# The front of a one-core attention and MLP kernel: four maximum products and six projection products in turn, and what stands behind the first closing

## The chip, the cores and the metric

The kernel runs on one core of a Trainium2 chip. The metric is device time in microseconds of one execution. The core has TensorE (matrix products, called PE in the profile), VectorE (DVE), ScalarE (ACT) and GpSimd (POOL); SyncE (SP) issues most transfers. The kernel writes the order of instructions in each of the five queues out by hand, and no scheduler changes it.

## The reference, cut to what matters

One block: a layer norm with shift and scale from a condition vector `c`, attention with 32 heads of 16 numbers that share one set of keys and values, a gated residual, a second layer norm, and an MLP with a tanh GELU. 2048 rows of 512 numbers, all in float32.

```python
mod = (_silu(c) @ w_mod).reshape(c.shape[0], 6, 1, -1)
sa, ca, ga, sb, cb, gb = (mod[:, 0], mod[:, 1], mod[:, 2], mod[:, 3], mod[:, 4], mod[:, 5])
h = _layernorm(x, axis=-1) * (1 + ca) + sa
q = ... (x @ wq) as 32 heads of 16; k = x @ wk; v = x @ wv
scores = jnp.einsum("bhqd,bkd->bhqk", q, k) * (Dh ** -0.5)
p = _softmax(scores, axis=-1)
x = x + ga * (p v as 512 numbers a row) @ wo
h = _layernorm(x, axis=-1) * (1 + cb) + sb
x = x + gb * (_gelu(h @ w1 + b1) @ w2 + b2)
```

## The kernel before, in words

**The attention.** A unit `u` is one block of 256 query rows with four heads. For each unit the scores are computed twice. The first time, 32 products `m<-ks,qst` (L512) give scores of 128 queries against 512 keys; VectorE reduces each to its row maximum (`mx<-m`, L517). When the 32 reduces of a unit are done, the unit is closed by `put_max`: one more reduce (`mm`, L565), a transpose (`turned`, L566), the gathering of the maxima into rows (`mt`, L560), the split of these into a high and a low part (`mh`, `ml`), and transfers that put both as rows 48 and 49 (and 112 and 113) of the unit's query tile `qst` (L555). The second time, products `e<-qst,ks` (L617) give the same scores with the maximum already subtracted, ScalarE takes the exponential (`p<-e`, L621), and `acc<-p,va` (L638) multiplies by the values. The products of units 0 and 1 are taken in the order of `FIRST_MAX`, over both units; unit 0 is complete with the 48th product. That is the first closing. The loop over units starts with an `e` of unit 0, so it needs the first rows to have landed.

**Halves of the array.** `m` and `e` contract over 64 rows. A product with `s` = 0 uses the upper half of the array and one with `s` = 1 the lower, so two of them run side by side. The projections contract over all 128 rows.

**The front.** Ahead of the loop the 2048 rows are normalised, transposed and modulated block by block of 512 (`tp`, `h`, `bigH`, `bigL`: "heads 1" to "heads 3"). From each block come the keys and values (`kps`, 12 products in four groups of three: "keys 1" to "keys 3"). ScalarE copies the keys out twice (`kv_out`, L401) and the values once (`vt`, L402), VectorE computes the keys' low part (`low_k`, L407), ScalarE copies this once more (`repeat_k`, L411), and `v_out` (L419, L420) transposes the values. "q 1" is the second projection of queries (`qps`, 12 products), "rows" the four sets of late modulation rows (`modl`, L297, 8 instructions each), "wq 1" to "wq 3" the split of query weights (L342, L343), "load" the loading of unit 2's queries.

The order of all this around the maximum products is a table, `SLOTS`. Each entry is a number of maximum products followed by names of steps. This loop reads it:

```python
for n, *names in SLOTS:
    chunk(n)
    for name in names:
        next(work[name])
```

Four more maximum products follow the table, so that 56 are issued when the loop begins.

**PSUM banks.** The kernel divides its PSUM into eight tiles of 512 numbers a partition. The maximum products take turns in three with the tag `m`. Three more, `e0` to `e2`, are given out in rotation by `ebank()`; in the front the transposes `tp` and `vps` use them, and in the loop the `e` products, beginning with `e0`. The remaining two have the tags `v` (`kps` of blocks 0 to 2, `qps` of "q 1") and `x` (`kps` of block 3, `modl`). A product waits until the engine that empties its bank has done so, and what stands behind it in TensorE's order waits with it.

**Idle products.** `keep_warm` issues products whose result nobody reads. `WARM` holds how many at four places; the last is straight ahead of the loop (L1410).

Of the kernel before, what the change touches and what calls it, by code (L numbers as in the profile page):

```python
# [14 lines left out]
P = 128  # L15
# [29 lines left out]
WARM = (4, 16, 2, 5)  # L45
# [4 lines left out]
def raw(ap):  # L50
    return ap.bitcast(F32)
# [3 lines left out]
def adaln_mqa_mlp(  # L55
# [230 lines left out]
    def keep_warm(n, **place):  # L286

        for k in range(n):
            if k == 0 or not place:
                ps = psum.tile([P, BQ], F32, name=f"idle{len(idles)}", **(place or dict(tag="m", bufs=3)))  # L290
                idles.append(ps)
            nc.tensor.matmul(ps, wkH[:, 0, :], wkH.rearrange("p k n -> p (k n)"), start=True, stop=True)
# [98 lines left out]
    def kv_products(b):  # L391
        hH, hL = hts[b]
        kps[b] = psum.tile([P, BQ], F32, name=f"kps{b}", tag="x" if b == 3 else "v")
        return mm3(kps[b], [(wkH[:, k, :], wkL[:, k, :], hH[:, k, :], hL[:, k, :]) for k in range(KD)], 3)

    def kv_out(b):
        ps = kps[b]
        cols = slice(b * BQ, (b + 1) * BQ)
        vt = pro.tile([P, BQ], F32, name=f"vt{b}", tag="vt", bufs=2)
        for r in range(2):  # L400
            nc.scalar.copy(ks[64 * r:64 * r + 48, cols], ps[64 * r:64 * r + 48, :])  # L401
        nc.scalar.copy(vt[32:64, :], ps[32:64, :])  # L402
        vts[b] = vt

    def low_k(b):
        cols = slice(b * BQ, (b + 1) * BQ)
        nc.vector.tensor_tensor(out=ks[32:48, cols], in0=kps.pop(b)[32:48, :], in1=raw(ks[32:48, cols]), op=ALU.subtract)  # L407
# [128 lines left out]
    def put_max(u, mx):  # L536
# [13 lines left out]
        def send():  # L550
            for s in range(2):
                for r, src in ((48, mh), (49, ml)):
                    dst = qst[64 * s + r:64 * s + r + 1].rearrange("p j (t n) -> p (j t) n", n=P)
                    ring = nc.scalar if u == 0 and s else nc.sync
                    ring.dma_start(out=raw(dst), in_=raw(src[2 * T * s:2 * T * (s + 1), :].unsqueeze(1)))  # L555
            placed.add(u)
# [7 lines left out]
        def reduce():  # L564
            nc.vector.tensor_reduce(out=mm[:, :4 * T], in_=mx, axis=AX.X, op=ALU.max)  # L565
            nc.vector.transpose(out=turned, in_=mm)  # L566
            later(MAX_WAIT[0], gather)
            later(MAX_WAIT[1], send)
# [676 lines left out]
    def k_products(b):  # L1245
        for _ in kv_products(b):
            pass
# [84 lines left out]
    run(keys(0))  # L1332
    low_k(0)
# [19 lines left out]
    for n, *names in SLOTS:  # L1353
        chunk(n)
        for name in names:
            next(work[name])
# [53 lines left out]
    keep_warm(WARM[3], tag="e2", bufs=1)  # L1410
# [172 lines left out]
```

## Time and profile before

| | us |
|---|---|
| three timed runs | 1555.87, 1556.47, 1556.48 (median 1556.47) |
| the profiled execution | 1555.99 |
| its span, first to last instruction | 1554.1 |
| PE busy | 1537.9 (99%) |
| DVE busy | 1398.3 (90%) |
| ACT busy | 1230.4 (79%) |
| POOL busy | 683.7 (44%) |
| first maximum reduce of the stretch that the change rewrites, start | 48.68 |
| first `e` product of the loop, start | 75.14 |

In the profile's rows a time stands first, then a duration; `x8` is the number of instructions that a row merges, and the brackets hold the engine's idle time before the row and what ended it. The duration of a merged row runs from the start of the first to the end of the last. Instructions of one engine can overlap at their ends, so rows that follow each other start a little closer together than their durations say. The granted clock of TensorE is 1.000 over the whole execution.

### The profile page before, as it was taken

To read this page: it belongs to the slowest core of one execution; us is meant where nothing else is said; L and a number is where in the kernel's file an instruction comes from. 1 tells how busy PE (TensorE), PEld (TensorE's weight loads), DVE (VectorE), ACT (ScalarE), POOL (GpSimd) and SP (SyncE) were. 2 spreads that over 40 slices of the span, in tenths; PEclk is the share of its full clock that TensorE was granted. 3 is DMA by queue.
4 is the path that set the end of the run, shared out by engine and by line. 5 is a ranking of instruction groups with operands and counts; after the bars stand their busy time and mean duration, and the time that the engine had idled before them with its cause. 6 is when DMAs were issued, how large, how long until landed. Compare 5 with 4: busy or idle time off the path is not lost.

```text
span 1554.1 us, 41556 instructions
## 1 busy us (share of the span) xinstructions
PE 1537.9 (99%) x16405; PEld 954.4 (61%) x16405; DVE 1398.3 (90%) x2488; ACT 1230.4 (79%) x2401; POOL 683.7 (44%) x1206
## 2 busy tenths in 40 slices
PE   7999999999999999999999999999999999999999
PEld 4455555567655665557655676556655676566658
DVE  7999999999999999999999999999999999999814
ACT  5577778788877887788877888788877888778874
POOL 5535432867422571246521563235711574046511
PEclk9999999999999999999999999999999999999999
DMA  7226412413030220303112120302212230203141
GB/s 240 102 89 199 151 57 81 130 51 97 18 105 26 72 68 28 103 19 109 33 51 79 56 87 16 111 26 88 68 30 73 60 101 25 87 28 99 48 150 48
DMA packets 84215, 120.85 MB, mean 78 GB/s; under 512 B 21342, under 2 KB 57438, under 8 KB 83764
## 3 DMA queue, kind: packets, MB, share of 16 engines
q1 hardware_dynamic: 84004, 118.18, 23.7%
q8 instruction: 130, 2.13, 0.6%
q14 instruction: 65, 0.53, 0.1%
q10 hardware_dynamic: 16, 0.00, 0.0%
HBM read 90.87 MB, written 26.74 MB: 76 GB/s over the span
## 4 chain that ended last, share of the span: by engine, by line
PE 86%; DVE 8%; issue 3%; POOL 2%; DMA 1%; ACT 0%; SPq 0%; POOLq 0%; DVEq 0%
PE acc L638 29%; PE m L512 23%; PE e L617 16%; PE w1ps L198 8%; DVE mx L517 6%; PE w2ps L198 2%; PE w2ps L188 2%; DMA xt<-in_A_x_dram 1%; PE w1ps L188 1%; PE wops L198 1%; PE tp L198 1%; PE qps L198 1%; PE kps L165 1%; DVE st L823 0%; DVE x L816 0%
## 5 line engine op out<-in xcount | busy, mean ns | idle before, releaser
L517 DVE TENSOR_REDUCE mx<-m 128x1 f32<-128x512 f32 x2048 | 1270.6, 682 | 86.6 <-PE m L512 65.1
L621 ACT ACTIVATE p<-e 128x512 f32<-128x512 f32 x2048 | 1098.8, 598 | 255.1 <-PE e L617 112.0
L512 PE MATMUL m<-ks,qst 64*128 64x512 f32 x2048 | 836.7, 429 | 2.0 <-DVE mx L517 0.6
L617 PE MATMUL e<-qst,ks 64*128 64x512 f32 x2048 | 740.2, 412 | 0.0
L638 PE MATMUL acc<-p,va 128*32 128x256 f32 x8192 | 548.0, 385 | 0.0
L512 PEld LDWEIGHTS m<-ks,qst 64*128 64x128 f32 x2048 | 368.2, 184 | 205.1 <-DVE mx L517 173.5
L617 PEld LDWEIGHTS e<-qst,ks 64*128 64x128 f32 x2048 | 359.6, 184 | 89.3 <-ACT p L621 62.5
L638 PEld LDWEIGHTS acc<-p,va 128*32 128x32 f32 x8192 | 214.0, 109 | 213.9 <-issue 110.9
L198 PE MATMUL w1ps<-h2H,w1t 64*128 64x256 f32 x1232 | 235.5, 287 | 0.0
L560 POOL TENSOR_SCALAR mt<-turned 8x32 f32<-8x32 f32 x256 | 53.1, 208 | 399.9 <-DVE turned L566 387.9
L198 PEld LDWEIGHTS w1ps<-h2H,w1t 64*128 64x128 f32 x1232 | 186.0, 185 | 28.9 <-DVE mx L517 14.8
L198 PE MATMUL w1ps<-h2L,w1t 64*128 64x256 f32 x616 | 169.3, 275 | 0.0
L198 PE MATMUL w2ps<-w2H,gH 64*128 64x512 f32 x274 | 120.3, 439 | 0.0
L198 PEld LDWEIGHTS w1ps<-h2L,w1t 64*128 64x128 f32 x616 | 114.1, 185 | 0.0
L198 PE MATMUL w2ps<-w2L,gH 64*128 64x512 f32 x274 | 107.5, 392 | 0.0
L198 PE MATMUL w2ps<-w2H,gL 64*128 64x512 f32 x274 | 106.9, 390 | 0.0
L975 POOL TENSOR_SCALAR tt<-tt 128x256 f32<-128x256 f32 x77 | 31.0, 402 | 131.5 <-ACT tt L974 96.5
L140 POOL TENSOR_TENSOR gL<-z,gH 128x256 fp32r<-128x256 f32 x77 | 57.0, 741 | 6.4
L976 POOL TENSOR_TENSOR tt<-tt,z 128x256 f32<-128x256 f32 x77 | 56.7, 736 | 6.4
L986 POOL TENSOR_TENSOR z<-tt,z 128x256 f32<-128x256 f32 x77 | 56.4, 732 | 6.0
L985 POOL TENSOR_TENSOR tt<-tt,z 128x256 f32<-128x256 f32 x77 | 56.5, 733 | 0.0
L198 PEld LDWEIGHTS w2ps<-w2H,gH 64*128 64x128 f32 x274 | 50.4, 184 | 6.7 <-DVE ot L1038 2.5
(193 smaller groups left out, 1503.5 us busy)
## 6 DMA issues: line engine op xcount, KB each, us to landing
w1t<-dw SPq DMA_DIRECT2D x82, 512.0 KB
qst<-dq SPq DMA_DIRECT2D x384, 32.0 KB
do<-oc SPq DMA_DIRECT2D x62, 128.0 KB
dw<-w1s SPq DMA_DIRECT2D x11, 512.0 KB
xt<-in_A_x_dram SPq DMA_DIRECT2D x4, 1024.0 KB
dq<-qH SPq DMA_DIRECT2D x16, 256.0 KB
dq<-qL SPq DMA_DIRECT2D x16, 256.0 KB
x<-in_A_x_dram SPq DMA_DIRECT2D x8, 512.0 KB
```

Of the source, the lines that this page charges most:

```text
L140: eng_l.tensor_tensor(out=dst_l, in0=src, in1=raw(dst_h), op=ALU.subtract)
L188: nc.tensor.matmul(ps, a, b_, start=first_, stop=last_)
L198: ins = nc.tensor.matmul(ps, a[rows], b_[rows], start=first_ and s == 0, stop=last_ and s == 1)
L512: nc.tensor.matmul(m, qsts[u][rows, j, t * P:(t + 1) * P], ks[rows, kc * 512:(kc + 1) * 512], start=True, stop=True)
L517: nc.vector.tensor_reduce(out=self.mx[u][:, i, kc:kc + 1], in_=m, axis=AX.X, op=ALU.max)
L560: nc.gpsimd.tensor_scalar(out=mt[:, g:g + 32], in0=turned[g:g + 4 * T, :], scalar1=1.0, scalar2=0.0, op0=ALU.mult, op1=ALU.add)
L617: nc.tensor.matmul(e, ks[rows, kt * P:(kt + 1) * P], rhs, start=True, stop=True)
L621: ins = nc.scalar.activation(dst, e, AF.Exp, scale=0.25)
L638: ins = nc.tensor.matmul(accs[u][32 * cidx:32 * cidx + 32, :], va[:, kt, :], rhs, start=kt == 0, stop=kt == NKT - 1)
L976: nc.gpsimd.tensor_tensor(out=tt, in0=tt, in1=z, op=ALU.mult)
L985: nc.gpsimd.tensor_tensor(out=tt, in0=tt, in1=z, op=ALU.mult)
L986: nc.gpsimd.tensor_tensor(out=z, in0=tt, in1=z, op=ALU.add)
```

## The change

It rewrites the table `SLOTS` and five things around it.

- An entry may now hold several numbers among its names. From the first keys of block 2 on, four maximum products stand in a row and then six projection products, where before two and three alternated.
- In these entries (from the 12th on, but for the last two) the odd ones of the maximum products, counted from 0 (`s` = 1), take a bank of the rotation `e0` to `e2` instead of one of the three `m`.
- The values `v 2` and `v 3`, all four sets of `rows`, and the query weights `wq 2` and `wq 3` stand behind the 48th product. Six products then follow inside the table in place of four, and two behind it in place of four.
- The copy `vt` of blocks 1 to 3 moves from `kv_out` to behind `repeat_k`, and is now called `keep_v`.
- The first unit's rows (`place_first`): two of the four pieces of `mt` are copied by ScalarE and two by GpSimd, `mh` is made by ScalarE and `ml` by GpSimd. Each of `mh` and `ml` is put in place by one transfer of two rows from SP, where there were four of one row, two of them from ScalarE.
- The five idle products ahead of the loop are gone (the last number of `WARM` is 0).

TensorE's order at the start of the rewritten stretch, in the program before (`kps` is a product of keys 2, `m_u_j_t_kc_s` a maximum product of the unit whose last numbers it shows):

```order
L165 MATMUL kps_646<-bigH,wkH 128x512
L165 MATMUL kps_646<-bigH,wkL 128x512
L165 MATMUL kps_646<-bigL,wkH 128x512
L512 MATMUL m_1_0_1_0_650<-ks,qst_157 128x512
L512 MATMUL m_1_0_1_1_653<-ks,qst_157 128x512
L165 MATMUL kps_646<-bigH,wkH 128x512
L165 MATMUL kps_646<-bigH,wkL 128x512
L165 MATMUL kps_646<-bigL,wkH 128x512
L512 MATMUL m_1_1_1_0_659<-ks,qst_157 128x512
L512 MATMUL m_1_1_1_1_662<-ks,qst_157 128x512
```

And in the changed program:

```order
L517 MATMUL m_1_0_1_0_646<-ks,qst_157 128x512
L517 MATMUL m_1_0_1_1_649<-ks,qst_157 128x512
L517 MATMUL m_1_1_1_0_652<-ks,qst_157 128x512
L517 MATMUL m_1_1_1_1_655<-ks,qst_157 128x512
L166 MATMUL kps_658<-bigH,wkH 128x512
L166 MATMUL kps_658<-bigH,wkL 128x512
L166 MATMUL kps_658<-bigL,wkH 128x512
L166 MATMUL kps_658<-bigH,wkH 128x512
L166 MATMUL kps_658<-bigH,wkL 128x512
L166 MATMUL kps_658<-bigL,wkH 128x512
```

The two pairs of maximum products moved together and stand ahead of the first projection products of keys 2.

TensorE's order around the first closing before; `m_1_1_3_1` is unit 0's last maximum product (`modl` are mod rows, `vps` the transposes of values, `qps` the last products of "q 1"):

```order
L165 MATMUL qps_1_754<-h0L,wqH 128x512
L297 MATMUL modl<-wml_0_378,csb 32x512 x2
L297 MATMUL modl<-wml_1_379,csb 32x512 x2
L512 MATMUL m_1_0_3_0_798<-ks,qst_157 128x512
L512 MATMUL m_1_0_3_1_801<-ks,qst_157 128x512
L419 MATMUL vps_804<-ident,vt_730 128x32 x4
L512 MATMUL m_1_1_3_0_814<-ks,qst_157 128x512
L512 MATMUL m_1_1_3_1_817<-ks,qst_157 128x512
L297 MATMUL modl<-wml_0_382,csb 32x512 x2
L297 MATMUL modl<-wml_1_383,csb 32x512 x2
L512 MATMUL m_0_0_2_0_842<-ks,qst_158 128x512
L512 MATMUL m_0_0_2_1_845<-ks,qst_158 128x512
```

And now:

```order
L166 MATMUL qps_1_754<-h0L,wqH 128x512
L517 MATMUL m_1_0_3_0_787<-ks,qst_157 128x512
L517 MATMUL m_1_0_3_1_790<-ks,qst_157 128x512
L517 MATMUL m_1_1_3_0_793<-ks,qst_157 128x512
L517 MATMUL m_1_1_3_1_796<-ks,qst_157 128x512
L424 MATMUL vps_815<-ident,vt_699 128x32 x4
L299 MATMUL modl<-wml_0_378,csb 32x512 x2
L299 MATMUL modl<-wml_1_379,csb 32x512 x2
L517 MATMUL m_0_0_2_0_826<-ks,qst_158 128x512
L517 MATMUL m_0_0_2_1_829<-ks,qst_158 128x512
L424 MATMUL vps_832<-ident,vt_752 128x32 x4
L299 MATMUL modl<-wml_0_382,csb 32x512 x2
```

The first set of mod rows and a set of value transposes left the way to the closing; both value transposes and all mod rows follow it.

ScalarE's order at the same place before (`turned` holds the transposed maxima, `q_0_1` and `qH` belong to "q 1", `modl_sb` is the copy of the mod rows):

```order
L135 CAST qH_1_785<-q_0_1_787 128x512
L420 COPY va<-vps_804 128x4x16
L342 CAST wqH<-wqf 128x4x64 x2
L555 DMA qst_157<-mh_824 1x4x128
L555 DMA qst_157<-ml_825 1x4x128
L342 CAST wqH<-wqf 128x4x64 x2
L1364 COPY modl_sb<-modl 128x512
```

And now:

```order
L136 CAST qH_1_779<-q_0_1_781 128x512
L564 COPY mt_802<-turned_799 8x32 x2
L136 CAST mh_803<-mt_802 8x128
L425 COPY va<-vps_815 128x4x16
L425 COPY va<-vps_832 128x4x16
L344 CAST wqH<-wqf 128x4x64 x4
L1387 COPY modl_sb<-modl 128x512
```

ScalarE lost two transfers and gained three small copies, ahead of the value copies and the weights.

The diff, without the parts that only rename:

```diff
-         (2, "heads 3"), ..., (0, "keys 2"), (2, "keys 2"), (2, "keys 2"), (2, "keys 2"),
+         (4, "keys 2", "keys 2"), (4, "keys 2", "keys 2"), (2, "low 2", 2, "k 2", "keys 3", "keys 3", "v 1", "wq 1"), ...
...
+WIDE = 11
-WARM = (4, 16, 2, 5)
+WARM = (4, 16, 2, 0)
...
     def kv_out(b):
-        vt = pro.tile([P, BQ], F32, name=f"vt{b}", tag="vt", bufs=2)
         for r in range(2):
             nc.scalar.copy(ks[64 * r:64 * r + 48, cols], ps[64 * r:64 * r + 48, :])
-        nc.scalar.copy(vt[32:64, :], ps[32:64, :])
-        vts[b] = vt
...
+    def keep_v(b):
+        vts[b] = pro.tile([P, BQ], F32, name=f"vt{b}", tag="vt", bufs=2)
+        nc.scalar.copy(vts[b][32:64, :], kps[b][32:64, :])
 
     def repeat_k(b):
         cols = slice(b * BQ, (b + 1) * BQ)
         nc.scalar.copy(ks[96:112, cols], raw(ks[32:48, cols]))
+        if b:
+            keep_v(b)
...
+        def place_first():
+            for i in range(2):
+                for g, piece in ((32 * i, lambda d, s: nc.scalar.copy(d, s)),
+                                 (64 + 32 * i, lambda d, s: nc.gpsimd.tensor_scalar(out=d, in0=s, ...))):
+                    piece(mt[:, g:g + 32], turned[g:g + 4 * T, :])
+
+            def send_row(r, src):
+                dst = qst[r:r + 65:64].rearrange("p j (t n) -> p (j t) n", n=P)
+                nc.sync.dma_start(out=raw(dst), in_=raw(src.unsqueeze(1)))
+
+            split(mh, ml, mt, nc.scalar, nc.gpsimd, lambda: send_row(48, mh))
+            send_row(49, ml)
+            placed.add(u)
...
         def reduce():
             nc.vector.tensor_reduce(out=mm[:, :4 * T], in_=mx, axis=AX.X, op=ALU.max)
             nc.vector.transpose(out=turned, in_=mm)
+            if u == 0:
+                place_first()
+                return
...
+    wide = [False]
     def chunk(n):
         for _ in range(n):
-            mp.step(mp.done % 2)
+            mp.step(mp.done % 2, **(ebank() if wide[0] and mp.done % 2 else {}))
...
-    for n, *names in SLOTS:
-        chunk(n)
-        for name in names:
-            next(work[name])
+    for i, slot in enumerate(SLOTS):
+        wide[0] = WIDE <= i < len(SLOTS) - 2
+        for part in slot:
+            if isinstance(part, int):
+                chunk(part)
+            else:
+                next(work[part])
```

More of the change, by code (lines that the diff above doesn't have):

```diff
@@ L284, in adaln_mqa_mlp, with keep_warm @@
     idles = []
-    def keep_warm(n, **place):
+    def keep_warm(n, src=None, **place):
+        src = wkH.rearrange("p k n -> p (k n)") if src is None else src
         for k in range(n):
@@ L291, in keep_warm @@
                 idles.append(ps)
-            nc.tensor.matmul(ps, wkH[:, 0, :], wkH.rearrange("p k n -> p (k n)"), start=True, stop=True)
+            nc.tensor.matmul(ps, src[:, :P], src, start=True, stop=True)
     def mod_rows(ps, k, wm):
@@ L1332, in adaln_mqa_mlp @@
     run(keys(0))
+    keep_v(0)
     low_k(0)
@@ L1408, in end_step @@
                 put_off(rest(units[u][0], units[u][0] == len(blocks) - 1))
-    keep_warm(WARM[3], tag="e2", bufs=1)
+    keep_warm(WARM[3], bigH[:, 0, 0, :], tag="v")
     behind = None
```

9 lines of the change are left out of this document (3 added, 6 removed), and 8 rows, old and new, of the table SLOTS.

## The prediction

> **What bounds the kernel now.** I read the chain that ended last first, then busy time by stage, then VectorE and TensorE in order of time through the front.
>
> ```profile
> PE 86%; DVE 8%; issue 3%; POOL 2%; DMA 1%; ACT 0%; SPq 0%; POOLq 0%; DVEq 0%
> ```
> ```profile
> 48.17:69.56 21.39, 21.11 (x92) 10.11 (x91) 19.12 (x30) 9.90 (x21) 10.13 (x11) 1.00 0.06 22
> ...
> 69.56:75.14 5.58, 5.26 (x29) 1.92 (x27) 5.33 (x10) 0.74 (x2) 2.81 (x10) 1.00 0.08 23
> ...
> 84.70:1450.00 1365.30, 1364.52 (x15160) 846.27 (x15160) 1280.62 (x2245) 1114.49 (x2172) 614.30 (x1091) 1.00 0.23 73
> ```
>
> In the second fence the columns are the stretch, its length, then busy time and instructions of PE, PEld, DVE, ACT and POOL, the granted clock, the DMA share and GB/s. From 84.70 to 1450 us TensorE idles under 1 us: that is the long loop, and the change leaves its instructions as they are. So the change can only move the start of that loop. The part it edits runs from 48.17 to about 84.7 us. There TensorE is busy 21.11 of 21.39 us and VectorE 19.12: two engines near their limit, each waiting a little for the other. VectorE in order of time:
>
> ```profile
> 48.68 5.27 DVE L517 TENSOR_REDUCE mx<-m 128x1 f32<-128x512 f32 x8 [0.51 <-PE m L512]
> 54.04 0.68 DVE L407 TENSOR_TENSOR ks<-kps,ks 16x512 fp32r<-16x512 f32 x1
> ...
> 54.76 5.21 DVE L517 TENSOR_REDUCE mx<-m 128x1 f32<-128x512 f32 x8
> 60.06 0.68 DVE L407 TENSOR_TENSOR ks<-kps,ks 16x512 fp32r<-16x512 f32 x1
> ...
> 67.05 2.48 DVE L517 TENSOR_REDUCE mx<-m 128x1 f32<-128x512 f32 x4 [1.05 <-PE m L512]
> 69.56 0.19 DVE L565 TENSOR_REDUCE mm<-mx 128x8 f32<-128x32 f32 x1
> ...
> 69.92 5.14 DVE L517 TENSOR_REDUCE mx<-m 128x1 f32<-128x512 f32 x8
> 75.91 7.27 DVE L517 TENSOR_REDUCE mx<-m 128x1 f32<-128x512 f32 x12 [0.85 <-PE m L512]
> ```
>
> I number the maximum products 1, 2, ... as they run; each has one reduce. Unhindered, twelve reduces take 7.27 us with a last one of about 0.68: one starts every 0.60 us. But the eight at 48.68 take 5.27, 0.65 each, since they come in pairs that wait for TensorE:
>
> ```profile
> 47.27 0.48 PE L165 MATMUL kps<-bigH,wkH 128*128 128x512 f32 x1
> ...
> 48.15 0.50 PE L512 MATMUL m<-ks,qst 64*128 64x512 f32 x2
> 48.58 0.51 PE L165 MATMUL kps<-bigH,wkH 128*128 128x512 f32 x1
> ...
> 49.15 0.40 PE L165 MATMUL kps<-bigL,wkH 128*128 128x512 f32 x1
> 49.47 0.50 PE L512 MATMUL m<-ks,qst 64*128 64x512 f32 x2
> ```
>
> A pair of products holds TensorE 0.43 us (48.15 to 48.58), three projection products 0.89 (48.58 to 49.47): 1.32 per pair, where VectorE needs 1.20. A pair that starts at 48.15 is reduced from 48.68, 0.53 later. So from 48.17 on TensorE sets the pace, until the first closing (product 48 reduced, row at 69.56). Behind it:
>
> ```profile
> 66.51 0.50 PE L512 MATMUL m<-ks,qst 64*128 64x512 f32 x2
> 66.94 0.43 PE L419 MATMUL vps<-ident,vt 32*128 32x32 f32 x4
> 67.30 0.98 PE L512 MATMUL m<-ks,qst 64*128 64x512 f32 x2
> 68.21 1.07 PE L297 MATMUL modl<-wml,csb 128*32 128x512 f32 x8
> 69.21 0.49 PE L512 MATMUL m<-ks,qst 64*128 64x512 f32 x2
> ...
> 73.75 1.47 PE L292 MATMUL idle<-wkH 128*128 128x512 f32 x5
> 75.14 0.49 PE L617 MATMUL e<-qst,ks 64*128 64x512 f32 x2
> 75.48 0.95 PE L512 MATMUL m<-ks,qst 64*128 64x512 f32 x2
> ```
>
> The first e, the loop's start, follows the five idle products without a gap: not the first rows but 1.39 us of idling ends last there.
>
> **The change part by part.** Four and six in turn. Once TensorE is in the half-array products, a product of each half goes every 0.23 us:
>
> ```profile
> 83.20 0.39 PE L617 MATMUL e<-qst,ks 64*128 64x512 f32 x1
> ...
> 83.43 0.39 PE L512 MATMUL m<-ks,qst 64*128 64x512 f32 x1
> ```
>
> I take 0.23 for the second pair and for each of three further projection products: 0.43 + 0.23 + 0.89 + 3 x 0.23 = 2.24 us per four, where two turns of before take 2.64. VectorE needs 2.40, so now it sets the pace. The odd products' banks (the three e banks) let TensorE run on: the fourth product of a turn waits only for the second of the turn before. One early turn doesn't gain: product 24 gets the bank of a heads transpose that ScalarE empties late:
>
> ```profile
> 47.48 0.78 ACT L386 ACTIVATE h<-tp,sa,ca 128x512 f32<-128x512 f32 x1 [0.46 <-POOL bigL L140]
> ...
> 52.23 1.19 ACT L401 CAST ks<-kps 48x512 fp32r<-48x512 f32 x2 [1.99 <-PE kps L165]
> ```
>
> It starts at 48.26, the six projections at 48.7, product 25 at 50.3, its reduce at 50.84; VectorE was free at 50.5: 0.35 lost. Later product 36 must wait for reduce 32, behind "low 2"; the six projections after it delay product 37 by 0.27. The remaining turns feed VectorE. The two "low" steps move two reduces later; ScalarE's two ks copies (1.19 us) before each, and its 16-row copy after each, lie beside queued reduces. The vt copies go behind it: the v transposes are far off, so nothing.
>
> The closing then: product 21 takes the place of the projections at 47.27, so its reduce follows the reduce before at once, at 48.1 (that one ends at 48.17). 28 reduces x 0.60 = 16.8, two low steps at 0.90 (52.66 + 1.2 would be the next reduce, 54.76 it is; the row of the pair stands here),
>
> ```profile
> 52.66 1.29 DVE L517 TENSOR_REDUCE mx<-m 128x1 f32<-128x512 f32 x2
> ```
>
> the two losses 0.62 and 0.09 of the last reduce's tail: 48.1 + 16.8 + 1.8 + 0.62 + 0.09 = 67.4 against 69.53 (67.05 + 2.48): 2.1 us earlier.
>
> Values, rows, weights behind the closing. Two value transposes (0.36 each, 66.94 to 67.30) and four sets of mod rows (1.00 each, 68.21 to 69.21) now stand between closing and loop, beside the same eight products; before it were two of the sets and no value. Loading unit 2 moves behind two of the products and costs nothing: its first product comes in the loop's second step. The v 3 transpose takes the bank of product 48, so TensorE waits for the closing, 67.45. From there 0.36 + 1.00, products 51 and 52 at 68.81, then 1.43 for each of the next two pairs: 70.24 and 71.67; the first e at 72.10, 3.0 earlier than 75.14. VectorE resumes at 67.79 (0.39 behind the closing as 69.92 is behind 69.53), and waits for those pairs 0.35, 0.23 and 0.23: reduces 51, 53 and 55 at 69.34, 70.77 and 72.20, and the loop's first, 57, at 73.40 (two more slots of 0.60) where it was 75.91: **2.5 us**. The wq preparations run on idle ScalarE and GpSimd; the loop's projections want them only behind its first acc (78.88 before).
>
> First rows by two engines. Before:
>
> ```profile
> 70.08 1.02 POOL L560 TENSOR_SCALAR mt<-turned 8x32 f32<-8x32 f32 x4 [0.33 <-DVE turned L566]
> 71.19 0.29 POOL L133 TENSOR_SCALAR mh<-mt 8x128 fp32r<-8x128 f32 x1
> ...
> 72.29 0.61 SPq L555 DMA_DIRECT2D qst<-ml  x1
> ...
> 72.96 0.59 ACTq L555 DMA_DIRECT2D qst<-ml  x1
> ```
> ```profile
> 44.17 0.21 ACT L420 COPY va<-vps 128x64 f32<-128x64 f32 x1
> ```
>
> mt starts 0.55 behind the closing: 67.95. Two pieces on GpSimd are half of 1.02, two on ScalarE about 2 x 0.21 beside them: 68.45. mh on ScalarE, unseen at this size, lies between 0.21 and the 0.62 of a 512-wide cast: 0.3, being nearest the first, so 68.8; the ml transfer can be issued 0.8 later, 69.6. Landing isn't shown; the last transfer before was issued at 72.96 and e ran at 75.14, so at most 2.18: 71.8, ahead of TensorE's 72.10. It is covered by the mod rows, and would cost nothing up to 72.6, since VectorE is behind e by 1.3 where it was by 0.8. Queued behind ScalarE's wait for mt are only the va and wq copies; SP holds two transfers instead of two plus two on ACT.
>
> The idle products, 1.39 us, go; what is late next is VectorE. The loop's first steps hold to it:
>
> ```profile
> 78.88 1.07 PE L638 MATMUL acc<-p,va 128*32 128x256 f32 x16
> ...
> 81.86 1.07 PE L638 MATMUL acc<-p,va 128*32 128x256 f32 x16
> ...
> 84.70 1.07 PE L638 MATMUL acc<-p,va 128*32 128x256 f32 x16
> ```
>
> 75.14 to 78.88 and 78.88 to 81.86 are 3.74 and 2.98 against 2.84 thereafter, and VectorE runs through twelve reduces without a gap. So e's 3.0 us counts only as VectorE's 2.5, and this shift then stays to the end.
>
> **Sum.** The profiled execution took 1555.99 us (span 1554.1); with the three timed runs (1555.87 to 1556.48, median 1556.47) the mean of the four is 1556.20. Less 2.5: **1553.7 us**.
>
> **Rivals.**
> *VectorE is never hungry.* If neither the 0.62 before nor the 0.81 after the closing is lost, the gain is 3.9: 1552.3. For it: both rest on single bank waits that I placed to a tenth. Against: the v 3 transpose really has product 48's bank.
>
> *The banks do not help.* If the later products of a four wait for the first's reduce, three reduces (1.80) must cover six projections and a new start (1.58 + 0.53): 0.31 lost in each of seven turns, 2.17 in place of 0.62. Gain 0.95: 1555.2. For it: TensorE's order is fixed, so a bank wait holds six projections now, not three.
>
> *The clock falls (slower).* Without the five idle products, and waiting more, TensorE might be granted half its clock at the loop's start. The two first steps hold 6.72 us, of which 1.04 is waiting for VectorE (3.74 + 2.98 - 2 x 2.84); the other 5.68 at half speed would take twice that, 4.6 more net: 1553.7 + 4.6 = 1558.3. It decides from 3.5 us of work at half speed (2.5 + 1.04). Against it: the granted clock reads 1.00 in all stretches, and after 1.25 us idle the next products run at 0.24:
>
> ```profile
> 27.61 0.66 PE L380 MATMUL tp<-ident,xt 128*128 128x128 f32 x4 [1.25 <-ACT h L386]
> 28.03 2.30 PE L292 MATMUL idle<-wkH 128*128 128x512 f32 x9
> ```
>
> The longest wait that I count in the new order is 0.7. The Trainium skill (TensorE: Matmul & The Clock Gate, sections HAM oscillation and A second HAM failure mode) says that an idle window of about 3.4 us halves the clock, and that many short waits on PSUM banks can too, which speaks against this change. By that rule one window at half speed would take an estimated 1.7 us, and the time would be near 1554.4. No row of this trace shows a halved clock.
>
> **How the numbers follow.** Forecast 0.60, VectorE never hungry 0.19, banks 0.13, clock 0.08. The likeliest case's own range is 1552.8 to 1554.6, some 0.9 us for bank waits and run spread; the range over all reaches from just under the second case to just over the third: 1552.0 to 1555.4. 0.2%, about what a measurement of this kernel can tell from no change, is 3.1 us: below 1553.36 is faster. The second case and some two fifths of the forecast lie there: 0.42. Slower by as much needs the clock to stay low beyond the two steps: 0.04. The rest is 0.54.
>
> **What would show it.** After: reduces at 0.60 from about 51 us on, closing near 67.4, one TensorE wait ahead of v 3, no idle products, first e near 72.1, first loop reduce near 73.4, then steps of 2.84. I am wrong if VectorE still waits in pairs before the closing, if the first e waits for the rows, or if the loop's period or the tail changes.

## The result, and the profile after

The changed kernel takes 1554.16 us (median of 21 runs, 1553.47 to 1555.40) beside 1556.63 for the kernel before (21 runs on the same chip). The ratio is 0.9984, 95% interval 0.9978 to 0.9990. The forecast was 1553.7 with a range of 1552.0 to 1555.4, "same" as the likeliest class and a gain of 2.5 us; measured were 2.47. The two agree more closely than the runs among themselves, so the last tenths of that are luck. The profiled execution took 1553.47 us (span 1551.7) where the one of before took 1555.99: 2.52 less.

VectorE in order of time after the change; the columns are as in the rows of before:

```profile
42.71 7.27 DVE L522 TENSOR_REDUCE mx<-m 128x1 f32<-128x512 f32 x12 [0.17 <-PE m L517]
50.67 3.68 DVE L522 TENSOR_REDUCE mx<-m 128x1 f32<-128x512 f32 x6 [0.69 <-PE m L517]
...
58.99 1.29 DVE L522 TENSOR_REDUCE mx<-m 128x1 f32<-128x512 f32 x2 [0.21 <-PE m L517]
...
61.02 6.07 DVE L522 TENSOR_REDUCE mx<-m 128x1 f32<-128x512 f32 x10
67.13 0.19 DVE L583 TENSOR_REDUCE mm<-mx 128x8 f32<-128x32 f32 x1
67.49 1.25 DVE L522 TENSOR_REDUCE mx<-m 128x1 f32<-128x512 f32 x2
69.05 11.30 DVE L522 TENSOR_REDUCE mx<-m 128x1 f32<-128x512 f32 x18 [0.31 <-PE m L517]
```

Before, eight reduces took 5.2 us because they came in pairs; now six take 3.68 and ten 6.07, 0.60 each. Two waits are left in the rewritten stretch ahead of the closing (0.69 and 0.21; the 0.17 at 42.71 lies before it), and the closing's `mm` stands at 67.13 where it stood at 69.56. The 18 reduces from 69.05 run into the loop; their last twelve are the loop's, so the first of these starts at 69.05 + 11.30 - 7.27 = 73.08, 2.83 earlier than 75.91.

TensorE after the change:

```profile
48.13 0.49 PE L517 MATMUL m<-ks,qst 64*128 64x512 f32 x1 [0.53 <-ACT h L388]
...
50.14 0.74 PE L517 MATMUL m<-ks,qst 64*128 64x512 f32 x4
...
52.40 0.73 PE L517 MATMUL m<-ks,qst 64*128 64x512 f32 x4
...
56.44 0.49 PE L517 MATMUL m<-ks,qst 64*128 64x512 f32 x1 [0.17 <-DVE mx L522]
...
67.15 0.43 PE L424 MATMUL vps<-ident,vt 32*128 32x32 f32 x4 [0.54 <-DVE mx L522]
...
71.69 0.40 PE L638 MATMUL e<-qst,ks 64*128 64x512 f32 x2
76.05 1.07 PE L659 MATMUL acc<-p,va 128*32 128x256 f32 x16
79.03 1.07 PE L659 MATMUL acc<-p,va 128*32 128x256 f32 x16
81.87 1.07 PE L659 MATMUL acc<-p,va 128*32 128x256 f32 x16
```

A turn of four and six products takes 52.40 - 50.14 = 2.26 us. All three bank waits that the prediction named are there: product 24 behind ScalarE (48.13), product 36 behind a reduce (56.44), and v 3 behind the closing (67.15). A fourth wait, which the prediction did not name (0.26 at 61.05, for "low 3"), costs nothing: VectorE's ten reduces from 61.02 follow without a gap. The first `e` follows at 71.69 without a wait. From there the steps are 4.36, 2.98 and 2.84: the third is the long loop's. By stage:

```profile
47.49:67.10 19.61, 17.74 (x80) 9.69 (x79) 18.57 (x31) 9.36 (x17) 9.43 (x10) 1.00 0.05 18
...
81.87:1447.17 1365.30, 1364.51 (x15163) 845.11 (x15162) 1280.84 (x2245) 1115.41 (x2173) 616.76 (x1091) 1.00 0.23 73
```

Ahead of the closing VectorE is now the fuller engine (18.57 of 19.61) and TensorE has slack (17.74); before it was TensorE with 21.11 of 21.39. The long loop, taken over a stretch of the same length, is what it was: 1364.51 busy of 1365.30 (before 1364.52). The last transfer of the first rows, in SP's queue:

```profile
69.28 0.53 SPq L570 DMA_DIRECT2D qst<-ml  x1
```

The last transfer is issued 2.15 us behind the closing's start (67.13), against 3.40 before (72.96 behind 69.56). By the trace's semaphores it has landed at 70.88, 0.81 ahead of `e`; before, the last row had landed at 74.60, 0.54 ahead of `e`.

**A start that moves.** Executions differ in when the front is under way. The first of the three low-key steps on VectorE (`ks<-kps,ks`), which the change hardly touches (it stands 0.08 behind the reduce ahead of it in before and 0.03 in after), shows it. It started at 38.74 in the profile of before and at 38.14 in that of after, so some of the 2.83 us is not the change. Two further profiles fill the gap: b_rows_only, before's program with only the rows' path changed, and a_idle5, the changed one with idle products; both are among the experiments. The first row is before's, the second the changed kernel's, then come two rows of b_rows_only and three of a_idle5.

```profile
38.74 0.68 DVE L407 TENSOR_TENSOR ks<-kps,ks 16x512 fp32r<-16x512 f32 x1
```
```profile
38.14 0.68 DVE L406 TENSOR_TENSOR ks<-kps,ks 16x512 fp32r<-16x512 f32 x1
```
```profile
38.10 0.68 DVE L407 TENSOR_TENSOR ks<-kps,ks 16x512 fp32r<-16x512 f32 x1
...
68.94 0.19 DVE L579 TENSOR_REDUCE mm<-mx 128x8 f32<-128x32 f32 x1
```
```profile
39.19 0.68 DVE L406 TENSOR_TENSOR ks<-kps,ks 16x512 fp32r<-16x512 f32 x1
...
51.23 3.68 DVE L522 TENSOR_REDUCE mx<-m 128x1 f32<-128x512 f32 x6 [0.22 <-PE m L517]
...
67.68 0.18 DVE L583 TENSOR_REDUCE mm<-mx 128x8 f32<-128x32 f32 x1
```

In the order of before, a start 0.64 earlier gives a closing 0.62 earlier (68.94 against 69.56). In the new order a start 1.05 later gives a closing only 0.55 later (67.68 against 67.13), since the wait of product 25's reduce shrinks from 0.69 to 0.22: product 24 waits for ScalarE's work on the heads, which moves less from run to run than VectorE does (product 24 starts at 48.69 there, 0.56 later than 48.13). Between the two, at before's own start of 38.74, I estimate a wait of 0.42, a closing at 67.4 and the loop's first reduce at 73.4. So at equal start the shift is 2.1 us at the closing and 2.5 in the loop, which is also what the medians show.

### The profile page after: what moved, and what is told of

Its sections match the earlier page's. It is cut to its first block, busy times and chain, and to the rows that moved or that the text cites. A ratio compares the mean times of both kernels' runs of the same rounds, so it can differ in the third digit from the quotient of the medians.

```text
span 1551.7 us, 41538 instructions
## 1 busy us (share of the span) xinstructions
PE 1534.5 (99%) x16400; PEld 952.6 (61%) x16400; DVE 1395.6 (90%) x2488; ACT 1232.1 (79%) x2404; POOL 685.7 (44%) x1203
## 4 chain that ended last, share of the span: by engine, by line
PE 84%; DVE 8%; issue 2%; POOL 2%; DMA 1%; SPq 1%; ACT 1%; POOLq 0%; DVEq 0%
PE acc L659 29%; PE m L517 23%; PE e L638 16%; PE w1ps L199 8%; DVE mx L522 7%; PE w2ps L199 2%; PE w2ps L189 2%; PE w1ps L189 1%; DMA xt<-in_A_x_dram 1%; PE qps L199 1%; PE wops L199 1%; PE tp L199 1%; POOL xt L375 1%; DVE st L844 0%; PE kps L166 0%
```

## Experiments

Each kernel ran eleven times, beside 33 runs of the kernel before on the same chip: a_no_wide, a_23, b_moved and a_idle5 on a first chip, b_warm0, a_old_place, a_cold and a_better on a second, the other four on a third (medians of before 1556.59, 1556.21 and 1556.64). Differences between kernels of different chips are taken by way of before. In some executions of nearly every program the mean granted clock of TensorE is below 1.000, and these are mostly 1 to 4 us longer. So the table gives the median of the eleven, the median of the runs with a clock of 1.000 less the same of before on that chip (1556.28, 1556.01, 1556.51), and how many had a lower clock (before: 18 of 99).

| kernel | median us | clock 1.000, against before | lower clock | ratio to before (95%) |
|---|---|---|---|---|
| a_no_wide | 1557.78 | +1.42 | 1 | 1.0008 (1.0000 to 1.0017) |
| a_23 | 1555.28 | -1.23 | 1 | 0.9990 (0.9982 to 0.9999) |
| b_moved | 1556.06 | -0.22 | 0 | 0.9997 (0.9988 to 1.0006) |
| a_idle5 | 1555.25 | -1.20 | 1 | 0.9989 (0.9980 to 0.9998) |
| b_warm0 | 1557.03 | -0.39 (one run) | 10 | 1.0003 (0.9994 to 1.0012) |
| a_old_place | 1553.81 | -2.28 | 1 | 0.9985 (0.9977 to 0.9994) |
| b_rows_only | 1556.04 | -0.54 | 2 | 0.9997 (0.9988 to 1.0006) |
| b_fast_rows | 1555.76 | -0.96 | 4 | 0.9995 (0.9986 to 1.0004) |
| a_cold | 1555.00 | none | 11 | 0.9995 (0.9987 to 1.0004) |
| a_again | 1554.59 | -2.47 | 2 | 0.9985 (0.9977 to 0.9994) |
| a_better | 1552.22 | -3.80 | 1 | 0.9976 (0.9967 to 0.9985) |
| a_better_again | 1553.01 | -3.51 | 2 | 0.9979 (0.9970 to 0.9988) |

The theory under test is the prediction's: VectorE fed at 0.60 per reduce brings the closing forward, and removing the idle products lets the loop's start follow. The rivals are that the extra banks do not matter, that the moves behind the closing do the work alone, that the rows' path or the idle products alone do it, and that the clock takes back what is won.

**a_no_wide: the change without the extra banks.**

```diff
-WIDE = 11
+WIDE = 99
```

> The changed kernel with every maximum product in the three m banks (WIDE past the table's end); four and six still in turn. The rival of the prediction (banks do not help) had 0.31 lost in each of seven turns: closing near 68.6 instead of 67.1 and 1555.7. Reckoned again from the changed kernel's rows: the fourth product waits for the first's reduce (0.53 + 0.69 after the turn begins), then its own 0.43 and six projections (1.58) run before the next turn, 3.26 a turn where VectorE needs 2.40; seven turns would put the closing near 70.5 to 71, and the time near 1557.5 to 1558, slower than the kernel before. If the e banks do nothing for the pace: 1554.2.

VectorE of this kernel in order of time:

```profile
51.24 2.48 DVE L522 TENSOR_REDUCE mx<-m 128x1 f32<-128x512 f32 x4 [0.81 <-PE m L517]
...
70.58 0.18 DVE L583 TENSOR_REDUCE mm<-mx 128x8 f32<-128x32 f32 x1
```

And its TensorE:

```profile
50.70 0.73 PE L517 MATMUL m<-ks,qst 64*128 64x512 f32 x3
51.99 0.50 PE L517 MATMUL m<-ks,qst 64*128 64x512 f32 x1 [0.55 <-DVE mx L522]
...
53.99 0.73 PE L517 MATMUL m<-ks,qst 64*128 64x512 f32 x3
```

With three banks the fourth product of a turn waits for the first's reduce, and the six projections wait with it. The turn is 53.99 - 50.70 = 3.29 us, VectorE idles 0.81 in it, and the closing comes at 70.58, later than before. So four and six in turn is a loss without the banks: it takes both. The closing is 3.45 us later than the changed kernel's (its first low-key step 0.46 later), and the time some 3.9 above it.

**a_23: the change with two and three in turn, without the extra banks.** The projections go back to turns of two maximum and three projection products; the moves behind the closing, the rows and the missing idle products stay as in the change.

```diff
-         (4, "keys 2", "keys 2"), (4, "keys 2", "keys 2"), (2, "low 2", 2, "k 2", "keys 3", "keys 3", "v 1", "wq 1"), (4, "keys 3", "keys 3"),
-         (2, "low 3", 2, "k 3", "q 1", "q 1"), (4, "q 1", "q 1"), (4, "v 2", "rows"),
-         (2, "v 3", "rows", "wq 2"), (2, "rows", "wq 3"), (2, "rows", "load"))
-WIDE = 11
+         (0, "keys 2"), (2, "keys 2"), (2, "keys 2"), (2, "keys 2"),
+         (2, "low 2", "k 2", "v 1", "wq 1"), (0, "keys 3"), (2, "keys 3"), (2, "keys 3"), (2, "keys 3"), (2, "low 3", "k 3"),
+         (2, "q 1"), (2, "q 1"), (2, "q 1"), (2, "q 1"), (2,),
+         (2, "v 2", "rows"), (2, "v 3", "rows", "wq 2"), (2, "rows", "wq 3"), (2, "rows", "load"))
+WIDE = 99
```

> The changed kernel with two products and three projections in turn again, in the three m banks; the values, rows and weights stay behind the first closing, the first rows stay by two engines, no idle products. Theory (the closing comes early because 2.7 us of TensorE work left the way to it, and VectorE then nearly keeps up): 14 pairs at 1.33 and one value transpose put product 47 at 65.4, VectorE lags by about half a microsecond behind the two low steps, closing 67.7 instead of 67.1: 0.6 lost, 1554.8. Rival (four and six in turn brings the gain): the closing goes back to about 69, 1556.

The first low-key step and the closing on VectorE of this kernel:

```profile
38.00 0.68 DVE L407 TENSOR_TENSOR ks<-kps,ks 16x512 fp32r<-16x512 f32 x1
...
67.67 0.19 DVE L584 TENSOR_REDUCE mm<-mx 128x8 f32<-128x32 f32 x1
```

The closing came at 67.67 with a start of 38.00, so 0.68 later than in the changed kernel at equal distance from its start, and the loop's first reduce (74.06 in the trace) 1.1 later. The time with a clock of 1.000 is about 1.2 us behind the changed kernel's, twice the 0.6 that was expected and less than the rival's loss. So turn and banks together are worth about 1.2 of the 2.5; the rest comes from what a_23 keeps, and is taken apart under b_fast_rows.

**b_moved: before, with only the moves behind the closing.** Turns, banks, rows and idle products are those of before.

```diff
-         (0, "v 2"), (2, "q 1"), (2, "q 1"), (2, "q 1"),
-         (2, "q 1", "rows"), (2, "v 3", "wq 2"), (2, "rows"), (2, "rows"), (2, "rows", "wq 3", "load"))
+         (2, "q 1"), (2, "q 1"), (2, "q 1"), (2, "q 1"), (2,),
+         (2, "v 2", "rows"), (2, "v 3", "rows", "wq 2"), (2, "rows", "wq 3"), (2, "rows", "load"))
```

> The kernel before with one part of the change alone: v 2, v 3, the four sets of rows, wq 2, wq 3 and load stand behind the 48th product. Two and three in turn, three m banks, first rows by GpSimd alone, five idle products. Theory: closing 67.8 instead of 69.5; behind it all four sets, both values and the idle products: first e near 73.7, first loop reduce near 74.5 where it was 75.91: 1.4 us gained, 1555.2. Rival (TensorE has the same work to do before the loop, so moving it gives nothing): 1556.6.

The closing on VectorE of this kernel, and TensorE ahead of its loop:

```profile
68.64 0.19 DVE L566 TENSOR_REDUCE mm<-mx 128x8 f32<-128x32 f32 x1
```
```profile
73.71 1.41 PE L293 MATMUL idle<-wkH 128*128 128x512 f32 x5
75.06 0.51 PE L618 MATMUL e<-qst,ks 64*128 64x512 f32 x2
```

The closing's `mm` came at 68.64, 0.9 earlier, but the first `e` only 0.08 earlier (75.06 against 75.14). My expectation missed here: I had counted the closing's gain and not that the moved work stands between closing and loop, on an engine that then still runs idle products for 1.41. Alone, the moves only change the place of TensorE's work.

**a_idle5: the change with the five idle products kept.**

```diff
-WARM = (4, 16, 2, 0)
+WARM = (4, 16, 2, 5)
```

> The changed kernel with the five idle products put back ahead of the loop, and nothing else. Theory (TensorE's own order ends last at the first e, VectorE sets the loop's first steps): the first e moves from 71.69 to 73.1, the loop's first reduce from about 73.1 (80.35 less twelve reduces in 7.27) to e + 0.77 = 73.85, so 0.8 us is lost: 1554.9 where the changed kernel has 1554.16. Rival (the first e waits for the rows to land, and the idle products only filled that wait): no change, 1554.2.

The idle products now read `bigH` and write to the bank `v`, where those of before read `wkH` and wrote to `e2`. TensorE and VectorE at the loop's start of this kernel:

```profile
72.34 1.42 PE L294 MATMUL idle<-bigH 128*128 128x512 f32 x5
```
```profile
74.45 7.26 DVE L522 TENSOR_REDUCE mx<-m 128x1 f32<-128x512 f32 x12 [0.72 <-PE m L517]
```

From closing to the loop's first reduce it takes 74.45 - 67.68 = 6.77 us where the changed kernel takes 73.08 - 67.13 = 5.95. So 1.42 us of idling cost 0.82 at the loop's start, as the prediction's "e's gain counts only as VectorE's" has it. The time is 1.2 to 1.3 us behind the changed kernel's, on other chips; the times alone do not tell 0.82 from the whole 1.42.

**b_warm0: before without the five idle products, and nothing else.**

```diff
-WARM = (4, 16, 2, 5)
+WARM = (4, 16, 2, 0)
```

> The kernel before with the five idle products ahead of the loop taken out, and nothing else. Theory (the first e stood behind idling, not behind the rows): e moves from 75.14 towards 73.75, as far as the rows have landed by then, which shows when they land; VectorE is through its eight reduces at about 75.0 and takes the first of the loop there instead of 75.91: 0.9 us gained, 1555.7. Rival (the rows landed only just before 75.14): nothing gained, 1556.6, and the trace shows TensorE idle ahead of e.

TensorE of this kernel around the loop's start:

```profile
73.74 0.57 PE L617 MATMUL e<-qst,ks 64*128 64x512 f32 x2 [0.66 <-DMA qst<-ml]
...
77.77 1.93 PE L638 MATMUL acc<-p,va 128*32 128x256 f32 x16
```

And its busy time in four stretches; the third column from the right is the granted clock:

```profile
76.00:77.00 1.00, 1.00 (x5) 0.54 (x5) 1.00 (x3) 1.00 (x3) 0.00 (x0) 0.69 0.17 42
77.00:78.00 1.00, 1.00 (x8) 0.49 (x10) 1.00 (x2) 0.91 (x3) 0.00 (x0) 0.50 0.11 26
78.00:79.00 1.00, 1.00 (x12) 0.39 (x8) 1.00 (x3) 0.51 (x1) 0.00 (x0) 0.50 0.00 0
79.00:80.00 1.00, 1.00 (x10) 0.36 (x4) 0.39 (x1) 0.00 (x0) 0.00 (x0) 0.60 0.00 0
```

Two things answered at once. TensorE was free at 73.08 and `e` waited 0.66 for the rows' landing: 73.74, where this execution's first low-key step came at 38.01, so at equal start only 0.67 earlier than before and not the 1.4 that the idle products took. And the granted clock fell to 0.50 for twice 0.31 + 0.50 + 0.50 + 0.40, so 3.42 us. Sixteen acc products took 1.93 in place of 1.07. Ten of eleven executions show a clock below 1.000; the one that does not took 1555.62, near the 1555.7 that I had expected of all, but only 0.39 less than before on that chip, where 0.9 was expected. So the idle products were not idle in effect: in the order of before, taking them away alone wins some 0.4 to 0.7, as far as one execution and one profile tell, and the clock takes it back. The Trainium skill (TensorE: Matmul & The Clock Gate, section Part 1: The HAM clock gate) says that the gate judges TensorE by free-running windows of about 3.4 us and, for a core that runs alone, has a full and a half state; the 3.42 us at 0.50 agree with one such window.

**a_old_place: the change with the rows of unit 0 made and sent as before.**

```diff
-                    nc.sync.dma_start(out=raw(dst), in_=raw(src[2 * T * s:2 * T * (s + 1), :].unsqueeze(1)))
+                    ring = nc.scalar if u == 0 and s else nc.sync
+                    ring.dma_start(out=raw(dst), in_=raw(src[2 * T * s:2 * T * (s + 1), :].unsqueeze(1)))
...
-            if u == 0:
-                place_first()
-                return
```

> The changed kernel with the first rows put in place as before: four pieces, both halves by GpSimd, four transfers, two of them from ScalarE. Theory (the rows are covered by the mod rows and by VectorE's lag): the last transfer is issued 3.4 us behind the closing at 67.1, so at 70.5, and lands between 1.2 and 2.18 later, 71.7 to 72.7; e waits up to 1.0 us, of which VectorE's lag (1.4 behind e, where 0.77 would do) hides 0.6: 0 to 0.4 us lost, 1554.2 to 1554.6. Rival (the faster rows are what brought the loop forward): the two steps saved, about 1.2 us from closing to the last issue, come back whole: 1555.4.

TensorE and VectorE of this kernel:

```profile
73.62 0.62 PE L636 MATMUL e<-qst,ks 64*128 64x512 f32 x2 [1.01 <-ACT wqH L344]
```
```profile
74.36 4.88 DVE L522 TENSOR_REDUCE mx<-m 128x1 f32<-128x512 f32 x8 [0.42 <-PE m L517]
```

The bracket names ScalarE's weight copy, whose semaphore changed last. But TensorE's queue stands in this `e`'s wait for the two row transfers of ScalarE's queue from 71.96 to 73.57, and the trace shows the second of them landed at 73.53; so it is the rows that `e` waits for. It comes 5.73 behind the closing (67.89) in place of 4.56, and VectorE's first loop reduce 74.36 - 67.89 = 6.47 behind it in place of 5.95. So in this execution the old path of the rows ends last, for 0.5 us.

This execution is not like the other ten. It is the one of eleven with a lower clock (0.50 from 75.77 to 79.18) and took 1555.74. The ten others, with a median of 1553.73, lost at most 0.2 to 0.3 against the changed kernel, within their spread: 1553.81 beside 1554.16 and 1554.59 on other chips is no loss at all. Whether they had the wait of 1.01 is not known, as none of them was profiled. That new rows are what the change lives on is refuted; that they are worth nothing isn't shown.

**b_rows_only and b_fast_rows: before with the new rows, and with them and without idle products.** Both add the changed kernel's `place_first`, called in `put_max` for unit 0; b_fast_rows has this line too:

```diff
-WARM = (4, 16, 2, 5)
+WARM = (4, 16, 2, 0)
```

> The kernel before with the first unit's rows by two engines alone; the five idle products stay, SLOTS as before. Theory: the idles end last ahead of e, the rows are covered, so nothing: 1556.2, clock 1.00. Rival (the rows' landing does end last in some runs behind the idles): up to 0.5 less, 1555.7.

> The kernel before with two edits alone: the first unit's rows made by ScalarE and GpSimd with two transfers from SP, and no idle products ahead of the loop. Its SLOTS are those of before. Theory (the rows' landing is what opened the idle gap ahead of e in the kernel before without idles, and that gap is what lets the granted clock halve): the last transfer is issued some 2 us earlier, e stands behind the mod rows without a gap near 73.7, no granted clock of 0.50 in most runs, the loop's first reduce 0.8 to 0.9 earlier than before: 1555.4. Rival (the halving comes from VectorE's pace at the loop's start, not from the wait for the rows): granted clock at 0.50 near 76 us again, about 1557.0, in most runs.

b_rows_only: no difference that can be told (0.9997, 0.9988 to 1.0006). The 0.54 of the table is the rival's size, but its profile shows no such gain: its `e` at 74.48 stands 36.38 behind the first low-key step, where before has 36.40. b_fast_rows, TensorE's first `e` and a stretch behind it:

```profile
73.89 0.62 PE L634 MATMUL e<-qst,ks 64*128 64x512 f32 x2
```
```profile
79.00:80.00 1.00, 1.00 (x16) 0.22 (x5) 1.00 (x3) 0.14 (x1) 0.00 (x0) 0.50 0.00 0
```

The wait for the rows is gone, and the seven executions with a clock of 1.000 win 0.96, as expected. But the clock still fell in four of eleven, the profiled one among them (0.50 from 78.47 to 81.89). So the gap ahead of `e` is likely a part of the cause (10 of 11 with it, 4 without); that VectorE's pace at the loop's start is the other part is the rival's view and not shown. That is between theory and rival, and with eleven runs each the size of either part is not settled.

The fall needs no wait for rows. The profile of a_23 is that of its one execution with a lower clock: 0.50 from 76.48 on, behind three microseconds (73 to 76) in which TensorE was busy 0.99, 0.90 and 0.83, in gaps of 0.10 at most. The changed kernel's profile shows nearly the same (0.99, 0.89 and 0.83 over 72 to 75, gaps of 0.11 at most) and keeps its clock. So gaps alone do not decide it, and what does stays open.

The parts of the change can now be set side by side. Counted from the first low-key step, the loop's first reduce (the ninth behind the closing) comes after 37.17 us in before, 36.21 in b_fast_rows, 36.06 in a_23 and 34.94 in the changed kernel; the table's medians at a clock of 1.000 are 0, 0.96, 1.23 and 2.47 (a_again) below before. So new rows with the idle products gone bring about 1.0, the moves 0.2 to 0.3 beside that (within the spread), turns and banks 1.1 to 1.2.

**a_cold: the change without the 16 idle products early in the front.**

```diff
-WARM = (4, 16, 2, 0)
+WARM = (4, 0, 2, 0)
```

> The changed kernel without the sixteen idle products ahead of the first maximum product as well, so that TensorE does nothing for nearly four microseconds at about 28 to 32 us. Theory (idle products cover waits and cost nothing, the clock stays up): 1554.2, products at the same pace after 32 us. Rival, the prediction's case of a falling clock, here provoked: the granted clock falls to half behind the idle stretch and the products after it run at twice the spacing for some microseconds: closing up to 1.7 later, 1555 to 1556.

TensorE of this kernel, and its busy times in a stretch ahead of these rows, with the granted clock third from the right:

```profile
32.19 0.79 PE L517 MATMUL m<-ks,qst 64*128 64x512 f32 x1 [2.26 <-ACT ks L414]
...
33.51 0.63 PE L166 MATMUL kps<-bigH,wkL 128*128 128x512 f32 x1
33.93 0.63 PE L166 MATMUL kps<-bigL,wkH 128*128 128x512 f32 x1
```
```profile
30.00:32.00 2.00, 0.00 (x0) 0.00 (x0) 1.80 (x2) 1.94 (x4) 1.37 (x2) 0.50 0.22 49
```

Every one of the eleven executions has a lower clock. Projection products go 0.42 apart in place of 0.23, and the time is 0.8 to 1.5 us behind the changed kernel's, by the medians against before on each chip. This is the clock rival brought about at another place: a clock at half from 29.7 to 36.6 us costs about 1. That it costs no more is probably because the products that slow down there have slack, which no run tested.

**a_again, a_better, a_better_again.** The prediction's bank waits can be placed elsewhere: the first turn of four becomes two turns of two, so that product 24 no longer holds six projections, and v 3 stands one entry later, so that the bank it takes has been read.

```diff
-         (4, "keys 2", "keys 2"), (4, "keys 2", "keys 2"), (2, "low 2", 2, "k 2", "keys 3", "keys 3", "v 1", "wq 1"), (4, "keys 3", "keys 3"),
+         (2, "keys 2", 2, "keys 2"), (4, "keys 2", "keys 2"), (2, "low 2", 2, "k 2", "keys 3", "keys 3", "v 1", "wq 1"), (4, "keys 3", "keys 3"),
...
-         (2, "v 3", "rows", "wq 2"), (2, "rows", "wq 3"), (2, "rows", "load"))
+         (2, "rows", "wq 2"), (2, "v 3", "rows", "wq 3"), (2, "rows", "load"))
```

> The changed kernel with two edits at the two waits that its trace shows: the first two turns of keys 2 go back to two products and three projections (product 24 then no longer holds six projections while ScalarE empties its bank), and v 3 goes behind products 51 and 52 (its bank is that of product 48). Theory: the 0.69 of idle VectorE at 50.67 goes to about 0.1, TensorE no longer waits 0.54 ahead of v 3, VectorE no longer 0.31 for product 51: closing 0.5 earlier, the loop's first reduce 0.9 earlier, 1553.3. Rival (the rows' landing takes over): e waits for the rows and half or more of that is lost, 1553.8 to 1554.2.

VectorE of a_better, and the transpose of v 3 on its TensorE:

```profile
42.69 11.01 DVE L522 TENSOR_REDUCE mx<-m 128x1 f32<-128x512 f32 x18 [0.17 <-PE m L517]
...
66.46 0.19 DVE L583 TENSOR_REDUCE mm<-mx 128x8 f32<-128x32 f32 x1
...
70.66 8.46 DVE L522 TENSOR_REDUCE mx<-m 128x1 f32<-128x512 f32 x14 [0.19 <-PE m L517]
```
```profile
67.29 0.43 PE L424 MATMUL vps<-ident,vt 32*128 32x32 f32 x4
```

The waits of 0.69 and of 0.54 are gone, that of 0.31 is 0.19; the closing comes at 66.46, 0.67 before the changed kernel's at an equal start. On the third chip both versions ran side by side.

> The changed kernel once more, to stand beside the better version on one chip: 1554.1, the loop's first reduce near 73.1, clock 1.00 in most runs.

> The version with the first entry of the new stretch as two turns of two and v 3 one entry later, once more beside the changed kernel: 1.2 us below it by the first look's rows (VectorE's waits of 0.69 and 0.31 gone), so 1552.9 where the changed kernel gives 1554.1. Rival (the difference between the two calls was the chip's): equal within 0.3.

1554.59 against 1553.01 (with a clock of 1.000: 1554.04 against 1553.00), so 1.0 to 1.6 us, as forecast from the rows. a_better is ahead of the kernel before on both chips, and of the changed kernel on the one where both ran; its ratio to the kernel before is 0.9976 (0.9967 to 0.9985) and 0.9979 (0.9970 to 0.9988).

## Why the prediction was right

*Closing, forecast 67.4.* Measured 67.13, and 67.4 at before's start by the estimate above. The steady reduces at 0.60 came as worked out. The waits were forecast at 0.35 and 0.27 and measured at 0.69 and 0.21; the first is larger because this execution's front ran 0.6 earlier while ScalarE's heads followed only in part. A low step was counted at 0.90 and takes 0.83 (a reduce could have started at 50.67 + 6 x 0.60 = 54.27 and starts at 55.10), since the 0.90 was read among pairs. That the 0.35 is a difference between two chains that vary separately, and not a constant, is what that step lacked.

*Behind the closing.* v 3's wait, the mod rows without a gap, and `e` at 72.10 (measured 71.69) held; VectorE's first wait was forecast at 0.35 and measured at 0.31; the two of 0.23 do not stand as rows, but the 18 reduces from 69.05 take 11.30 where 18 at 0.60 and a tail of 0.09 would take 10.89. The loop's first reduce was forecast at 73.40 and measured at 73.08, estimated 73.4 at equal start. That `e`'s gain counts only as VectorE's is what the rows show: `e` came 3.45 earlier (75.14 to 71.69), the third acc product group only 2.83 (84.70 to 81.87), as much as VectorE's reduce; and in a_idle5 1.42 of idling cost 0.82 there.

*Rows covered.* They landed at 70.88, ahead of 71.69, so nothing waited; the bound of 2.18 from issue to landing was 1.60. The profile of a_old_place shows the wait that the old path can bring: `e` 1.17 later behind the closing, VectorE's loop 0.52 later. So 0.65 was covered, where the prediction had allowed for 0.5.

*VectorE never hungry (1552.3).* It did not happen, since the waits are real; a_better shows that two of them can be had back for 1.0 to 1.6.

*The banks do not help (1555.2).* They do. And the price was wrong: 0.31 per turn by the prediction's sum, 0.81 measured in a_no_wide. The turn took 3.29 and VectorE needs 2.40. The sum let the six projections start with the first reduce's end and left out the fourth product's own half microsecond (0.50 at 51.99), which stands between the two.

*The clock falls.* In the sum it had 0.08 and 4.6 us net. Five of the 32 executions of the changed kernel show a clock below 1.000 (1555.09 to 1555.40), some 1.0 to 1.3 above the others, and 18 of 99 of the kernel before, so the change neither brings it nor ends it. The step of this rival that failed is the price: two whole steps at half speed were taken, where one stretch of 3.42 us is what the profiles of b_warm0, b_fast_rows, a_23 and a_old_place show at the loop's start. One such stretch loses 1.71 us of full clock in some 1552, a mean of 0.999, and two make 0.998 (a_cold's profile). All five executions of the changed kernel read 0.999, so I estimate one stretch in each, while 14 of the 18 of before read 0.998 or 0.997, two or three. Where in the program these lie isn't known: none of them was profiled. By the Trainium skill's rule (the page and sections named in the prediction) the estimate was one window of 1.7 us and 1554.4; the runs agree with the one window, and come out 0.7 to 1.0 above that time. And "against it: the granted clock reads 1.00 in all stretches" was a weak reason: one profiled execution of before says nothing on executions that were not profiled, nor on an order without the idle products. b_warm0 shows that taking out the idle products alone, in the order of before, brings it nearly always.

*End of the program.* The loop's shift arrives at the end but for about 0.4: 2.83 at its start and 2.4 between the spans. The last part's products go in two paces in both profiles (below), at different places. Nor is the long loop the same in every execution: the profile of a_again, the changed kernel once more, has its first `e` at 71.71, 0.02 behind, and its last acc product 1.04 later (1505.11 against 1504.07). So single profiles agree to about a microsecond at their ends, and the 2.5 rests on the medians.

## What to carry to other kernels

Where two engines alternate in small groups, compare the turn's time on each. A longer turn helps only with banks for the whole group: the in-order queue otherwise holds everything behind the first bank wait. Work that is moved out of the way of one wait gains nothing while padding at its new place still ends last. Padding that "does nothing" may be what holds the clock, so it is tried by itself and over many executions, not by one profile; and a single profile may be of the odd execution, so its clock is read first. A wait between two chains that start apart has no fixed size; place the product so that neither waits.

## What the runs showed of the hardware

The clock's fall has a length: 3.42 us in the profiles of b_warm0, b_fast_rows, a_23 and a_old_place, and twice that in a_cold (0.93, 0.50, 0.50, 0.50 and 0.86 over 28 to 30, 30 to 36 and 36 to 38 us). It does not need a long gap: in b_warm0 TensorE was busy 1.00 in each of the two microseconds ahead of it, behind a wait of 0.66.

At a granted clock of 1.00 the same 256-wide products run in two paces. In the last part of before, and of after:

```profile
1520.47 0.40 PE L188 MATMUL w1ps<-h2H,w1t 128*128 128x256 f32 x2
...
1525.24 0.39 PE L188 MATMUL w1ps<-h2H,w1t 128*128 128x256 f32 x2
```
```profile
1517.51 0.40 PE L189 MATMUL w1ps<-h2H,w1t 128*128 128x256 f32 x2
...
1522.46 0.40 PE L189 MATMUL w1ps<-h2H,w1t 128*128 128x256 f32 x2
```

Each pair of rows spans 14 groups of three products: 4.77 us in before, 4.95 in after, so 0.114 against 0.118 per product. Both paces occur in both profiles at other places, and a_again, the program of after, runs this stretch of 132 products at 0.113. So it is not the program that sets the pace. What does is open; it takes back about half a microsecond here and is a part of the run spread.
